# Tile 0's norm ahead of tile 1's sums, B and C from ScalarE's queue, and new prices for the planner

## The chip, the cores and the metric

The kernel runs on one core of a Trainium2 chip. The metric is the device time of one execution in microseconds (us), the median of several runs; lower is better.

## The reference

Three stages follow each other, for 4 sequences of 768 positions, in fp32:

```
# 1. scan attention, 8 heads, head size 32, state 16
la = log(clip(a)); cum = cumsum(la)             # per chunk of 32 positions
M = (C @ B.T) * exp(cum_i - cum_j) * causal
y = M @ x + (C @ state) * exp(cum)
state = exp(sum la) * state + (B * decay).T @ x
# 2. gated FFN on y (model size 256, inner size 1536)
xn = y / sqrt(mean(y*y) + 1e-6) * rms_g
z = (silu(xn @ w_gate) * (xn @ w_val)) @ w_out
# 3. channel mix on z (inner size 1024)
xk, xr = mixes of z with z one position earlier, by mu_k and mu_r
out = sigmoid(xr @ w_r) * (relu(xk @ w_k)**2 @ w_v)
```

The kernel uses chunks of 128 positions instead of 32, which gives the same sums. The weights are 64-bit floats in DRAM.

## The kernel before

**Tiles.** The 768 positions are six tiles of 128; a tile holds that stretch of all 4 sequences, so 512 columns. For each tile t the kernel runs `ffn1(t)`, the gated FFN in 12 units of 128 inner columns, and `ffn2(t - 1)`, the channel mix in 8 units; between their units it places the attention of tile t+1. Each unit of `ffn1` makes `g` and `v` (six matmuls each: weights and activations are split into a high and a low fp32r part, and `mm3` at L671 to L673 multiplies three of the four pairs), then Silu on ScalarE (`tabled`), the product `hf` on VectorE (L702), its high part by a cast on ScalarE (L137) and its low part by a subtraction on VectorE (L140). Two units later `contract` multiplies it with `w_out`. Tile 0's attention and norm have no FFN to stand beside, so they come first.

**Tile 0.** `load_a4` and `logs_e` fetch and clip `a` and take its logarithm; `sums_e(c)` on VectorE makes running sums and the small factors that `spread_e` multiplies on TensorE into a matrix of log decays (`Eb`), to which a matmul with `eye` adds the causal mask; `exp_e` takes its exponential on ScalarE (tile `E`). This is done for tiles 0 and 1 (c = 0, 1), four sequences each, two halves per sequence. `scores` multiplies C and B (L456, fp32), `masked` multiplies scores and decays (L492), `y_mm` makes y and the new state, `y_out` copies y to SBUF, `rms_sq` and `rms_mm` square it and sum over the features, `rms_a`, `rms_rest`, `rms_b` compute 1/rms on tiny tiles (Ln, Exp, Square on ScalarE, three small operations on VectorE), a matmul spreads it (L647), and `xn_f` and `xn_split` make the FFN's input `xn` and its two parts. The norm is done in two halves of 256 columns (`cols`), by `norm0`.

**Weights.** Each of 27 jobs is a block of 64-bit floats (512 KB); two jobs share a staging tile `wst` of two buffers. `convert` turns a pair into fp32r parts by bit operations: a clamp on VectorE (`move`, L260), two activations on ScalarE (`magnitude`, L265 and L267), a shift-and-or on VectorE (`merge`, L271), and per job a cast on ScalarE (L280) and a subtraction on VectorE (L281). Jobs 3q, 3q+1 and 3q+2 are w_gate, w_val and w_out for units 2q and 2q+1. `first` and `second` are jobs 0 to 3; after them `need(NEED[t][u])` places a pair before unit u of tile t as soon as that due time exceeds the number done.

**Activation tables.** Ln and Exp share one table of ScalarE, Silu and Sigmoid each have one; a switch is an instruction of its own (L124). `tabled` inserts it and chains every table function and every switch to the one before it in the program's order.

**Order.** The order on each engine is not the program's. `Order` takes all instructions, their dependencies and a price for each (`price`), and runs a list scheduler: whenever an engine is free, it takes the ready instruction that stands earliest in the program, if its buffers are free. `SIGNAL`, `LANDING` and `RATE` are its delays between engines, after a DMA, and its DMA rate in bytes per ns. The order so found is written into the program by `arrange`; on the chip each engine then runs its list in order. So a place earlier in the program is a higher rank, and a wrong price leaves an engine waiting at the head of its list. `warm_up` writes matmuls of ones that nobody reads; as they are always ready, they fill TensorE's waits.

The changed stretch of the program, before:

```
for b in range(NB): exps(0, b)
scores(0, 0); scores(0, 1)
sums_e(1)
for b in range(NB): ...       # masked, y_mm, y_out, sums of squares, state
exps(1, 0); exps(1, 1)
for s in cols: norm0(s)
for step in first: step()
exps(1, 2); exps(1, 3)
warm_up(WARM[1], pacc, "acc")
for step in second: step()
```

Of the kernel before, what the change touches and what calls it, by code (L numbers as in the profile page):

```python
# [16 lines left out]
P = 128  # L17
# [18 lines left out]
NEED = ((6, 6, 6, 10, 10, 12, 12, 14, 16, 16, 18, 18, 18),  # L36
# [7 lines left out]
WARM = (16, 24)  # L44
# [32 lines left out]
def tile_kernel(ctx: ExitStack, tc, a_c, x_t, B_t, B_s, C_s, B_p, C_p, C_h, kc,  # L77
                w_gate, w_val, w_out, w_k, w_v, w_r, out):
    nc = tc.nc
    slots, chains, groups = {}, [], []  # L80
# [38 lines left out]
    tab = [None, None]  # L119

    def tabled(out, in_, func, **kw):
        want, ins = TABLES.get(func, tab[1]), []
        if tab[1] != want:
            ins.append(lambda: nc.scalar.preload_act_table_set(want))  # L124
        ins.append(lambda: nc.scalar.activation(out=out, in_=in_, func=func, **kw))  # L125
        for make in ins:
            if tab[0] is None:
                tab[0] = make()
            else:
                nxt = make()  # L130
                chains.append((tab[0].ins.name, nxt.ins.name))
                tab[0] = nxt
        tab[1] = want

    def split(x, src, he, le):
        if he is act_e:
            nc.scalar.copy(x[:, 0, :], src)  # L137
        else:
            nc.vector.tensor_copy(x[:, 0, :], src)
        last[0] = le.tensor_tensor(out=x[:, 1, :], in0=src, in1=f32(x[:, 0, :]), op=ALU.subtract).ins  # L140

    last = [None]
# [198 lines left out]
    def sums_e(c):  # L341
        ln, w = a4[:, c], t2("hv", F32R)
# [16 lines left out]
    def spread_e(c, b):  # L359
        for half in range(2):  # L360
            ps = A[c]["Eb", b, half] = pmm.tile([P, T], F32, tag="mm", name="Eb")
# [39 lines left out]
    def load_b0():  # L401
        r = pair("xn", "Br", F32).rearrange("p a b -> p (a b)").rearrange("p (b k i) -> p b k i", b=NB, k=2)
        nc.sync.dma_start(out=r[:64], in_=B_p[0].rearrange("r b (k i) -> r b k i", k=2))
# [3 lines left out]
    def load_c0(b):  # L407
        r = A[0]["Cr", b] = rp.tile([P, 4, P], F32, tag="Cr" if b < 2 else "Br", bufs=2, name="Cr")
        nc.sync.dma_start(out=r[:64], in_=C_p[0, b].rearrange("r (k i) -> r k i", k=4))
# [173 lines left out]
    def rms_sq(c, s, he, le):  # L583
        d = A[c]
        if c <= 1:
            q = t2("sq").rearrange("p (a i) -> p a i", a=2)[:, :, :s.stop - s.start]
# [63 lines left out]
    def xn_f(c, half, s):  # L650
        d = A[c]
        f = d["xnf", half, s.start] = t2("xnf")[:, s]
# [152 lines left out]
    nc.sync.dma_start(out=k_sb, in_=kc)  # L805
    load_a4(1)
    warm_up(WARM[0], patt, "at")
    load_c0(0)
    load_b0()
    load_x(0, 1)  # L810
    load_c0(1)
    load_x(0, 0)
    load_c0(2)
    load_c0(3)
    for _ in range(2):
        w_load()
    first, second = steps(), steps()
    for c in range(2):
        logs_e(c)
# [8 lines left out]
    sums_e(0)  # L828
# [4 lines left out]

    for b in range(NB):
        exps(0, b)
    scores(0, 0)
    scores(0, 1)
    sums_e(1)
    for b in range(NB):
# [5 lines left out]
        if b % 2:  # L845
            rms_sq(0, cols[b // 2], act_e, vec_e)
            rms_mm(0, cols[b // 2])
# [403 lines left out]
```

## Time and profile before

| | |
|---|---|
| median of 3 runs | 533.36 us (530.85 to 533.69) |
| profiled execution | 529.57 us, of it span 527.8 us |
| TensorE (PE) busy | 518.5 us, 98% |
| VectorE (DVE) busy | 381.7 us, 72% |
| ScalarE (ACT) busy | 311.1 us, 59% |
| bytes moved by DMA | 42.34 MB |

Busy time of matmuls is that of pipelined records with modelled ends, so 98% does not mean that TensorE is at its peak: a 512-column matmul has a record of 0.39 us, while the next one starts 0.23 us later. L137 is line 137 of the kernel. "Idle before" in a row is the time the engine stood before it, and after the arrow what ended that.

### The profile page before, as it was taken

What the parts mean: (1) busy time and instruction counts of PE and PEld (TensorE: products, weight loads), DVE (VectorE), ACT (ScalarE), POOL (GpSimd) and SP (SyncE); (2) the same over time, 40 slices, a digit from 0 to 9 for tenths busy, and PEclk for the clock granted to TensorE, in tenths of its full rate; (3) what the DMA queues carried; (4) which work ended last, traced back from release to release, by engine and by line L of the source; (5) the groups of instructions that cost most, each with busy time, mean ns of one, the idle gap of its engine ahead of it and who ended that gap; (6) DMA issues with size and microseconds to landing.
All of it is one profiled execution on the core that took longest, in us unless ns stands there. A gap on an engine that the chain in (4) does not pass through costs nothing.

```text
span 527.8 us, 7526 instructions
## 1 busy us (share of the span) xinstructions
PE 518.5 (98%) x2872; PEld 417.9 (79%) x2872; DVE 381.7 (72%) x628; ACT 311.1 (59%) x507; POOL 13.1 (2%) x28
## 2 busy tenths in 40 slices
PE   9999999999999999999999999999999999999997
PEld 5677777788887888888888887888888888888885
DVE  7789978997969585779995687986445863335772
ACT  3698758667548954356764355874437663245552
POOL 4000000000010000001000001000000000000000
PEclk9999989999999999999999999999999999999999
DMA  7845574444151011324011324011000010000001
GB/s 214 255 147 187 195 245 160 135 145 131 55 186 39 22 51 52 108 76 154 20 45 52 105 73 145 2 40 41 0 1 1 0 40 2 0 1 0 24 18 40
DMA packets 21923, 42.34 MB, mean 80 GB/s; under 512 B 2096, under 2 KB 5168, under 8 KB 21888
## 3 DMA queue, kind: packets, MB, share of 16 engines
q1 hardware_dynamic: 19584, 33.48, 19.4%
q10 hardware_dynamic: 2304, 8.39, 4.9%
q8 instruction: 22, 0.36, 0.3%
q14 instruction: 13, 0.11, 0.1%
HBM read 38.52 MB, written 3.34 MB: 79 GB/s over the span
## 4 chain that ended last, share of the span: by engine, by line
PE 84%; DMA 5%; ACT 3%; DVE 3%; SPq 1%; issue 1%; POOL 0%; ACTq 0%; DVEq 0%
PE v L673 10%; PE v L672 10%; PE v L671 10%; PE g L671 6%; PE g L672 6%; PE g L673 6%; PE x L673 5%; PE x L671 5%; PE x L672 5%; PE kp L671 4%; PE kp L673 4%; PE kp L672 4%; DMA wst<-in_w_v 2%; PE y L505 2%; DVE E L423 2%; DMA E<-la_r 2%
## 5 line engine op out<-in xcount | busy, mean ns | idle before, releaser
L702 DVE TENSOR_TENSOR hf<-sl,v 128x512 f32<-128x512 f32 x72 | 49.2, 683 | 51.8 <-PE v L673 47.7
L137 ACT CAST h<-hf 128x512 fp32r<-128x512 f32 x72 | 44.5, 619 | 64.9 <-DVE hf L702 64.9
L125 ACT ACTIVATE sl<-g 128x512 f32<-128x512 f32 x72 | 42.6, 593 | 43.7 <-PE g L673 43.4
L140 DVE TENSOR_TENSOR h<-hf,h 128x512 fp32r<-128x512 f32 x72 | 49.4, 687 | 24.2 <-ACT h L137 24.1
L671 PE MATMUL g<-xn,wgh 128*128 128x512 f32 x144 | 58.4, 406 | 2.3 <-ACT xn L137 1.3
L672 PE MATMUL g<-xn,wgl 128*128 128x512 f32 x144 | 56.8, 395 | 0.0
L673 PE MATMUL x<-h,woh 128*128 128x512 f32 x144 | 55.6, 391 | 1.2 <-DVE h L140 1.2
L673 PE MATMUL g<-xn,wgh 128*128 128x512 f32 x144 | 56.6, 393 | 0.0
L671 PE MATMUL x<-h,woh 128*128 128x512 f32 x144 | 56.3, 391 | 0.0
L671 PE MATMUL v<-xn,wvh 128*128 128x512 f32 x144 | 56.2, 391 | 0.0
L672 PE MATMUL x<-h,wol 128*128 128x512 f32 x144 | 56.2, 390 | 0.0
L673 PE MATMUL v<-xn,wvh 128*128 128x512 f32 x144 | 56.2, 390 | 0.0
L672 PE MATMUL v<-xn,wvl 128*128 128x512 f32 x144 | 56.2, 390 | 0.0
L140 DVE TENSOR_TENSOR h<-k,h 128x512 fp32r<-128x512 f32 x48 | 32.8, 686 | 11.3 <-ACT h L137 10.8
L775 DVE TENSOR_TENSOR k<-rl 128x512 f32<-128x512 f32 x40 | 29.8, 750 | 14.7 <-ACT rl L771 14.5
L137 ACT CAST h<-k 128x512 fp32r<-128x512 f32 x48 | 29.8, 620 | 15.7 <-DVE k L775 15.5
L673 PE MATMUL v<-h,wvvh 128*128 128x512 f32 x96 | 37.6, 391 | 0.4 <-DVE h L140 0.4
L423 DVE TENSOR_TENSOR_SCAN E<-E,cmask 128x1024 f32<-128x1024 f32 x16 | 36.6, 2285 | 1.8 <-DMA E<-la_r 1.6
L671 PE MATMUL kp<-xm,wkh 128*128 128x512 f32 x96 | 37.7, 393 | 0.0
L673 PE MATMUL kp<-xm,wkh 128*128 128x512 f32 x96 | 37.4, 390 | 0.0
L672 PE MATMUL kp<-xm,wkl 128*128 128x512 f32 x96 | 37.4, 389 | 0.0
L672 PE MATMUL v<-h,wvvl 128*128 128x512 f32 x96 | 37.4, 389 | 0.0
(148 smaller groups left out, 1015.7 us busy)
## 6 DMA issues: line engine op xcount, KB each, us to landing
E<-la_r ACTq DMA_DIRECT2D x16, 512.0 KB
x<-in_x_t SPq DMA_DIRECT2D x6, 512.0 KB
wst<-in_w_gate SPq DMA_DIRECT2D x6, 512.0 KB
wst<-in_w_val SPq DMA_DIRECT2D x6, 512.0 KB
wst<-in_w_out SPq DMA_DIRECT2D x6, 512.0 KB
Br<-in_B_s SPq DMA_DIRECT2D x12, 256.0 KB
Cr<-in_C_s SPq DMA_DIRECT2D x12, 256.0 KB
out<-r SPq DMA_DIRECT2D x12, 256.0 KB
```

Source lines behind the costliest of these rows:

```text
L125: ins.append(lambda: nc.scalar.activation(out=out, in_=in_, func=func, **kw))
L137: nc.scalar.copy(x[:, 0, :], src)
L140: last[0] = le.tensor_tensor(out=x[:, 1, :], in0=src, in1=f32(x[:, 0, :]), op=ALU.subtract).ins
L423: nc.vector.tensor_tensor_scan(out=e, data0=e, data1=cmask, initial=0.0, op0=ALU.mult, op1=ALU.max)
L505: nc.tensor.matmul(y[half][32 * j:32 * j + 32, at[half]:at[half] + P], x[:, b, h * D:(h + 1) * D], m[:, h, :], start=start and at[half] == ...
L671: nc.tensor.matmul(ps, w[0][:, k, ws], x[:, 0, :], start=first, stop=False)
L672: nc.tensor.matmul(ps, w[1][:, k, ws], x[:, 0, :], start=False, stop=False)
L673: nc.tensor.matmul(ps, w[0][:, k, ws], x[:, 1, :], start=False, stop=last)
L702: nc.vector.tensor_mul(hf, sl, v)
L775: nc.vector.tensor_mul(k2, rl, rl)
```

## The change

The program around tile 0 gets another order; the planner gets other prices; some tiles other buffers. `tabled` chains a table function to its table's load only, and a load to all users of the table before it. `gates` makes every VectorE and ScalarE instruction that stands behind the early load of Silu's table wait for the last two operations of tile 0's xn.

```diff
...
-NEED = ((6, 6, 6, 10, 10, 12, 12, 14, 16, 16, 18, 18, 18),
+NEED = ((4, 4, 6, 8, 10, 12, 12, 14, 16, 16, 18, 18, 18),
         (99, 99, 99, 99, 99, 99, 99, 99, 99, 99, 99, 99, 99))
...
 MEANS = (7, 10)
-WARM = (16, 24)
+WARM = (16, 12)
...
-    tab = [None, None]
+    tab = [None, None, []]
+
+    def table(func):
+        want = TABLES.get(func, tab[1])
+        if tab[1] != want:
+            load = nc.scalar.preload_act_table_set(want).ins.name
+            chains.extend((one, load) for one in tab[2])
+            if tab[0] and not tab[2]:
+                chains.append((tab[0], load))
+            tab[:] = load, want, []
     def tabled(out, in_, func, **kw):
-        want, ins = TABLES.get(func, tab[1]), []
-        if tab[1] != want:
-            ins.append(lambda: nc.scalar.preload_act_table_set(want))
-        ins.append(lambda: nc.scalar.activation(out=out, in_=in_, func=func, **kw))
-        for make in ins:
-            if tab[0] is None:
-                tab[0] = make()
-            else:
-                nxt = make()
-                chains.append((tab[0].ins.name, nxt.ins.name))
-                tab[0] = nxt
-        tab[1] = want
+        table(func)
+        one = nc.scalar.activation(out=out, in_=in_, func=func, **kw).ins.name
+        if tab[0]:
+            chains.append((tab[0], one))
+        tab[2].append(one)
...
         if he is act_e:
-            nc.scalar.copy(x[:, 0, :], src)
+            last[1] = nc.scalar.copy(x[:, 0, :], src).ins
         else:
-            nc.vector.tensor_copy(x[:, 0, :], src)
+            last[1] = nc.vector.tensor_copy(x[:, 0, :], src).ins
         last[0] = le.tensor_tensor(out=x[:, 1, :], in0=src, in1=f32(x[:, 0, :]), op=ALU.subtract).ins
-    last = [None]
+    last = [None, None]
...
     def sums_e(c):
-        ln, w = a4[:, c], t2("hv", F32R)
+        ln = a4[:, c]
+        w = rp.tile([P, T], F32R, tag="rs", bufs=1, name="hv") if c else t2("hv", F32R)
         hi, v = w[:, :P], w[:, P:2 * P]
...
         for half in range(2):
-            ps = A[c]["Eb", b, half] = pmm.tile([P, T], F32, tag="mm", name="Eb")
+            pool, tag = (pacc, "acc") if c else (pmm, "mm")
+            ps = A[c]["Eb", b, half] = pool.tile([P, T], F32, tag=tag, name="Eb")
             nc.tensor.matmul(ps, eye, before.unsqueeze(1).broadcast_to([P, 4, P]), start=True, stop=False)
...
-    def load_b0():
+    def load_b0(q):
         r = pair("xn", "Br", F32).rearrange("p a b -> p (a b)").rearrange("p (b k i) -> p b k i", b=NB, k=2)
-        nc.sync.dma_start(out=r[:64], in_=B_p[0].rearrange("r b (k i) -> r b k i", k=2))
+        q.dma_start(out=r[:64], in_=B_p[0].rearrange("r b (k i) -> r b k i", k=2))
         for b in range(NB):
...
-    def load_c0(b):
+    def load_c0(b, q=nc.sync):
         r = A[0]["Cr", b] = rp.tile([P, 4, P], F32, tag="Cr" if b < 2 else "Br", bufs=2, name="Cr")
-        nc.sync.dma_start(out=r[:64], in_=C_p[0, b].rearrange("r (k i) -> r k i", k=4))
+        q.dma_start(out=r[:64], in_=C_p[0, b].rearrange("r (k i) -> r k i", k=4))
...
         if c <= 1:
-            q = t2("sq").rearrange("p (a i) -> p a i", a=2)[:, :, :s.stop - s.start]
+            q = rp.tile([P, T], F32, tag="Ch", bufs=1, name="sq") if s.start else t2("sq")
+            q = q.rearrange("p (a i) -> p a i", a=2)[:, :, :s.stop - s.start]
         else:
...
     nc.sync.dma_start(out=k_sb, in_=kc)
+    warm_up(WARM[0], patt, "at")
+    load_c0(0, nc.scalar)
+    load_b0(nc.scalar)
+    load_c0(1, nc.scalar)
+    w_load()
+    load_x(0, 1)
+    load_c0(2)
+    load_x(0, 0)
+    load_c0(3)
     load_a4(1)
-    warm_up(WARM[0], patt, "at")
-    load_c0(0)
-    load_b0()
-    load_x(0, 1)
-    load_c0(1)
-    load_x(0, 0)
-    load_c0(2)
-    load_c0(3)
-    for _ in range(2):
-        w_load()
+    w_load()
     first, second = steps(), steps()
-    for c in range(2):
-        logs_e(c)
+    logs_e(0)
+
     def norm0(s):
...
-    sums_e(0)
     def exps(c, b):
...
+    sums_e(0)
+    scores(0, 0)
+    scores(0, 1)
     for b in range(NB):
         exps(0, b)
-    scores(0, 0)
-    scores(0, 1)
-    sums_e(1)
     for b in range(NB):
...
             rms_mm(0, cols[b // 2])
+            norm0(cols[b // 2])
         st_up(0, b)
-    exps(1, 0)
-    exps(1, 1)
-    for s in cols:
-        norm0(s)
+    edge = [i.name for i in last]
+    logs_e(1)
+    sums_e(1)
     for step in first:
         step()
-    exps(1, 2)
-    exps(1, 3)
-    warm_up(WARM[1], pacc, "acc")
+    for b in range(NB):
+        exps(1, b)
+    table(AF.Silu)
+    here = list(nc.cur_bb.bb.instructions)[-1].name
+    gates.extend((x, here) for x in edge)
+    warm_up(WARM[1], patt, "at")
     for step in second:
...
 class Order:
-    SIGNAL, LANDING, RATE = 90.0, 1900.0, 270.0
-
-    def __init__(self, instructions, slots, chains, groups):
+    SIGNAL, LANDING, RATE = 34.0, 2100.0, 300.0
+
+    def __init__(self, instructions, slots, chains, groups, gates):
         self.slots, self.ins = slots, []
...
             self.before[b].add(a)
+        for a, b in ((where[a], where[b]) for a, b in gates):
+            for k in range(b + 1, n):
+                if self.eng[k] == self.eng[a]:
+                    self.before[k].add(a)
         self.tiles, self.touch = [[] for _ in range(n)], {}
...
         if kind == "InstDMACopy":
-            return (380.0 if e == SP_ else 100.0), 0.0, False
+            return (600.0 if e == SP_ else 100.0), 0.0, False
         if e == PE_:
...
             if x.dtype == F32:
-                part = 0.3 if aps[0].ap[0][1] <= 32 else 0.55 if x.ap[0][1] <= 64 else 1.0
-                return 20 + 1.7 * n * part, 200.0, False
-            return (228.5 if n >= T else max(n / 2.4 + 15, 45.0)), 180.0, False
+                rows, k = aps[0].ap[0][1], x.ap[0][1]
+                if k == P:
+                    return (15 + 0.32 * n if rows <= 32 else max(220.0, 20 + 1.7 * n)), 170.0, False
+                return 20 + 0.95 * n, 170.0, False
+            return (228.0 if n >= T else max(n / 2.4 + 13, 45.0)), 165.0, False
+        inputs = [a for a in i.ins if hasattr(a, "bass_ap")]
+        each = sum(columns(a) == 1 for a in inputs) if n > 1 else 0
         if e == ACT_:
-            return (1280.0, 0.0, False) if kind == "InstLoadActFuncSet" else ((60 + 0.94 * n if n > P else 250.0), 100.0, False)
+            if kind == "InstLoadActFuncSet":
+                return 1285.0, 0.0, False
+            return max((0.97 * n if kind == "InstActivation" else 32 + 0.965 * n) + 95 * each, 115.0), 98.0, False
         two = kind == "InstTensorTensor" or getattr(i, "is_scalar_tensor_tensor", False)
         if e == POOL_:
-            return (100 + 2.3 * n, 50.0, True) if kind == "InstTensorTensor" else (100 + 0.5 * n, 50.0, False)
+            return (150 + 2.5 * n, 60.0, True) if kind == "InstTensorTensor" else (80 + 0.95 * n, 60.0, False)
         if kind == "InstMemset":
             return 60.0, 30.0, False
-        psum = any(self.slots.get(a.bass_ap.tensor.name, ("",))[0] == "PSUM" for a in i.ins if hasattr(a, "bass_ap"))
+        psum = any(self.slots.get(a.bass_ap.tensor.name, ("",))[0] == "PSUM" for a in inputs)
         if getattr(i, "is_tensor_tensor_scan", False):
-            return 20 + 2.22 * n, 70.0, True
-        return 75 + (1.03 if two or psum else 0.52) * n, 75.0, not psum
+            return 48 + 2.1 * n, 82.0, True
+        return 73 + (1.035 if two or psum else 0.52) * n + 58 * each, 82.0, not psum
...
                 serial += 1
-                heapq.heappush(events, (t + self.cost[k][1] + self.SIGNAL, serial, k, [j for j in after[k] if eng[j] != e]))
+                heapq.heappush(events, (t + self.cost[k][1] + self.SIGNAL, serial, k,
+                                        [j for j in after[k] if eng[j] != e or e != PE_]))
                 for j in after[k]:
-                    if eng[j] == e:
+                    if eng[j] == e == PE_:
                         release(j)
...
```

## Rows read from the trace of the kernel before

**Rows 1.** The page's first part: busy us, share of span, instructions.

```profile
PE 518.5 (98%) x2872; PEld 417.9 (79%) x2872; DVE 381.7 (72%) x628; ACT 311.1 (59%) x507; POOL 13.1 (2%) x28
```

**Rows 2.** Stretches: length, busy us (count) by engine, granted clock, DMA share, GB/s.

```profile
0.00:5.00 5.00, 3.95 (x9) 3.14 (x10) 2.14 (x8) 1.69 (x3) 4.13 (x14) 1.00 0.29 67
5.00:10.00 5.00, 5.00 (x22) 2.84 (x20) 4.82 (x14) 0.84 (x3) 0.25 (x3) 1.00 0.98 290
10.00:15.00 5.00, 5.00 (x29) 2.47 (x30) 3.29 (x7) 3.61 (x7) 2.24 (x4) 1.00 1.00 357
39.40:64.00 24.60, 24.59 (x107) 18.14 (x108) 23.23 (x37) 19.76 (x28) 0.00 (x0) 1.00 0.62 205
72.00:74.00 2.00, 1.39 (x10) 1.08 (x9) 1.19 (x4) 1.97 (x5) 0.00 (x0) 0.90 0.88 246
74.00:77.50 3.50, 3.50 (x10) 2.84 (x11) 3.50 (x5) 1.40 (x4) 0.00 (x0) 0.57 0.96 360
```

**Rows 3.** Timeline of TensorE: start, us, line, operation, idle before.

```profile
1.05 5.92 PE L802 MATMUL warm<-ones 128*128 128x512 f32 x16 [1.05 <-DVE carry L862]
7.78 1.13 PE L456 MATMUL sc<-Cr,Br 32*128 32x256 f32 x6
14.42 0.43 PE L505 MATMUL y<-M,x 128*32 128x128 f32 x8
31.75 0.39 PE L671 MATMUL g<-xn,wgh 128*128 128x512 f32 x1
40.91 0.39 PE L671 MATMUL v<-xn,wvh 128*128 128x512 f32 x1
72.92 1.26 PE L612 MATMUL ss<-ones,sq 128*128 128x1 f32 x8 [0.61 <-ACT sq L589]
101.22 0.50 PE L671 MATMUL g<-xn,wgh 128*128 128x512 f32 x1 [1.32 <-ACT xn L137]
162.16 0.72 PE L673 MATMUL x<-h,woh 128*128 128x512 f32 x2 [1.18 <-DVE h L140]
```

**Rows 4.** Timeline of ScalarE, the same columns.

```profile
9.37 1.09 ACT L125 ACTIVATE E<-Eb 128x512 f32<-128x512 f32 x2 [4.16 <-PE Eb L363]
16.44 0.37 ACT L524 COPY yT<-y 128x256 f32<-128x256 f32 x1 [2.32 <-PE y L511]
18.59 0.63 ACT L589 ACTIVATE sq<-yT 128x512 f32<-128x512 f32 x1
25.14 0.26 ACT L125 ACTIVATE tiny<-ss,k_sb 128x2 f32<-128x2 f32 x1
28.68 1.58 ACT L137 CAST xn<-xnf 128x256 fp32r<-128x256 f32 x4 [0.18 <-DVE xnf L653]
30.16 1.08 ACT L125 ACTIVATE E<-Eb 128x512 f32<-128x512 f32 x2
32.16 2.22 ACT L267 ACTIVATE wst<-wst 128x1024 int32<-128x1024 uint32 x2
36.44 1.28 ACT L124 ACT_TABLE_LOAD   x1
37.73 0.62 ACT L280 CAST wvh<-wt 128x512 fp32r<-128x512 f32 x1
38.77 1.08 ACT L125 ACTIVATE sl<-g 128x512 f32<-128x512 f32 x2
69.74 0.34 ACTq L324 DMA_DIRECT2D E<-la_r  x1
```

**Rows 5.** Timeline of SP's queue, one issue.

```profile
3.99 0.58 SPq L320 DMA_DIRECT2D x<-in_x_t  x1
```

**Rows 6.** Timeline of VectorE.

```profile
3.04 0.91 DVE L183 TENSOR_SCALAR a<-a 128x128 f32<-128x128 f32 x1 [2.03 <-DMA a<-in_a_c]
7.76 0.42 DVE L344 TENSOR_TENSOR_SCAN a<-ones,a 128x128 f32<-128x128 f32 x1
11.19 1.28 DVE L492 TENSOR_TENSOR M<-sc,E 128x512 f32<-128x512 f32 x2
```

More of the change, by code (lines that the diff above doesn't have):

```diff
@@ L79, in tile_kernel @@
     nc = tc.nc
-    slots, chains, groups = {}, [], []
+    slots, chains, groups, gates = {}, [], [], []
     class Pool:
@@ L651, in xn_f @@
         d = A[c]
-        f = d["xnf", half, s.start] = t2("xnf")[:, s]
+        if s.start == 0:
+            d["xnf", half] = t2("xnf")
+        f = d["xnf", half, s.start] = d["xnf", half][:, s]
         nc.vector.scalar_tensor_tensor(out=f, in0=columns_of(c, s)[:, half], scalar=g_v[:, half:half + 1],
@@ L988, in tile_kernel @@
     ffn2(NC - 1, lambda *_: None)
-    arrange(tc, list(nc.cur_bb.bb.instructions), slots, chains, groups)
+    arrange(tc, list(nc.cur_bb.bb.instructions), slots, chains, groups, gates)
 ENGINES = (mybir.EngineType.PE, mybir.EngineType.DVE, mybir.EngineType.Activation, mybir.EngineType.Pool,
@@ L1200, in run, with arrange @@
         return t, order
-def arrange(tc, instructions, slots, chains, groups):
-    o = Order(instructions, slots, chains, groups)
+def arrange(tc, instructions, slots, chains, groups, gates):
+    o = Order(instructions, slots, chains, groups, gates)
     _, order = o.run()
```

## The prediction

> **What bounds the kernel now.** I read the page first: TensorE is busy 98% of the span [rows 1]. That is an average over stages with different limits, so next came the stretches [rows 2], and there the first 101 us stand apart. In all but two of these rows the clock is at its upper level, 2.4 GHz (1.00), and TensorE's records are dense, but until 31.75 us no FFN matmul runs: what fills TensorE is attention work for tile 0 and warm-up matmuls that nobody reads. The first FFN matmul starts at 31.75, and unit 2's second half, the first that needs weights of job 4, at 40.91 [rows 3]. Then I followed ScalarE through that time [rows 4]. Tile 0's exponentials start at 9.37; its norm (the `tiny` rows) waits until 25.14 behind tile 1's first exponentials; tile 1's last ones run at 30.16; three conversions' halves follow, then the switch to Silu's table at 36.44, a weight cast at 37.73, and the first Silu at 38.77. From about 25 us to there ScalarE hardly stops, so its queue sets when unit 2 can start, and TensorE's early units 0 and 1 only wait for it. Behind it VectorE is busy 23.23 of 24.60 us from 39.4 to 64 [rows 2]: little room there for work pushed later. Past 101 us TensorE is the limit; I found single stops before 101.22 (1.32 us) and 162.16 (1.18 us) [rows 3]. So only the first 101 us, with some 8 to 10 us of slack, can change much.
>
> **The change part by part.** The sum is against the profiled execution, 529.57 us (span 527.8 and 1.8 around it); the median of the three timed runs, 533.36, lies 3.8 above it. I carry the difference over to the median.
>
> *Loads.* B and C of tile 0 (C0, B0, C1: 512 KB) move from SP's queue to ScalarE's, and go out at once; SP sends two 512 KB weight blocks ahead of x. An issue on SP at the start took 0.58 us [rows 5], one on ScalarE's queue later 0.34 [rows 4]: three cost ScalarE 1.0 to 1.7 us ahead of its table load of 1.28, which then ends by 0.73+1.7+1.28 = 3.7. The first Ln waits for a clip on VectorE that began at 3.04 and took 0.91 [rows 6], so it starts at 3.95 at the earliest: the issues are hidden, and without that cover cost at most 1.7. x lands later: 67 GB/s over the first 5 us are 335 KB, then it ran at 290 GB/s, later 357 [rows 2]; 2.18 MB stand up to the end of x where 1.07 MB did, which makes 10.2 to 11.4 us instead of 7.5. The first matmul that reads x ran at 14.42 [rows 3] and in the new order may want it at about 12, so: nothing, at most 0.5 us. B's early landing is worth nothing by itself, since the 16 warm-up matmuls hold TensorE until 6.8 [rows 3].
> The DMA engines' share was 0.98 to 1.00 from 5 to 15 us [rows 2], on one queue. The Trainium skill, "DMA: Bandwidth & Descriptors", section "Issuing engines are not separate DMA queues", says that a second issuing engine only saves issue time because all queues share the 16 engines; the full share agrees, and it speaks against this part of the change: by it, and by the rows alike, the loads' term is zero.
>
> *Scores ahead of the exponentials, tile 1's sums behind.* Two blocks of scores at about 1.06 us each (six of their eight records took 1.13 with the pipeline's tail [rows 3]) now run right after the warm-up: 6.8+2.1, plus four fills of 0.23, gives 9.9, and the first exponential starts at 10.3, not 9.37. That is 0.9 lost. VectorE's second round of sums, from 7.76, ended only where the first masking product starts, at 11.19 [rows 6]; they go behind, so the first product follows its exponential at about 10.9. Masking itself thus hardly starts earlier, but its four pairs need not wait for scores again.
>
> *Norm first, then the table, then the rest.* No instruction vanishes; ScalarE's order does. I add up what ScalarE must do from tile 0's first exponential to the cast of job 4's weights, by [rows 4]: 16 exponentials at 0.54 (8.6), 4 copies of y at 0.37, 2 squares at 0.63, 6 small norm steps at 0.26, the xn casts 1.58, 6 conversion halves at 1.11 (6.7), 5 weight casts at 0.62 (3.1), the table 1.28: 25.6. About 17 of these are single records that overlap their neighbour by some 0.09 (two exponentials take 1.08, one 0.60): 24.1. Before, that list ran from 9.37 to 38.35, 29.0 us, so 4.9 us were idle. Now the Silus of units 0 and 1 (1.08) and their two casts (1.1) come ahead of job 4, because the due times move jobs 4 and 5 from unit 0 to unit 2: 24.1+2.2 = 26.3. From 10.3 that gives 36.6 plus idle time, and the subtraction on VectorE 0.7: unit 2's second half at 37.3 plus idle, against 40.91. With no idle time 3.6 are gained; with 4.9 again, 1.3 are lost. I take 0.9 idle, nearer the lower end, since the table-function chain that forced the old order is gone (Ln and Exp wait now only for their table load) and tile 1's exponentials and conversions can fill the norm's gaps: **-2.7**. The FFN itself may start at about 25 instead of 31.75, which by itself is worth nothing: units 0 and 1 then wait for Silu.
>
> *Gates.* VectorE's and ScalarE's work listed after the early table load now waits for tile 0's last xn. Behind it stand the state products, tile 1's decay clip, scan and product, some 3.5 us that VectorE did at 17 to 26. They fall into the stretch where VectorE had 1.4 us free in 24.6 [rows 2]. Much of it is due only with tile 1's y around 68; I price it at nothing, up to 3.5 (the rival below).
>
> *Prices.* The planner's order changes everywhere. Visible targets: the half-speed stretch 74 to 77.5, clock 0.57, costs 3.5x0.43 = 1.5, with 0.2 more in 72 to 74 [rows 2], and the wait of 0.61 before the sums of squares at 72.92 [rows 3] in front of it: 2.3 together. ScalarE had put a conversion half ahead of the copy and square these sums need. Truer prices may take that away or make another such place, 0 to -2.3, or +2.3 in the worst case: **-1.5**. Of the two later stops (2.5), which hang on a 2.3 us scan and a late load, I count **-0.7** (0 to -2.5). The smaller second warm-up (12 for 24) takes nothing from the path; its matmuls only filled waits. The tiles that get other buffers remove waits I see none of: nothing either way.
>
> Sum: -2.7-1.5-0.7 = **-4.9**: 524.7 for a profiled execution like this one, **528.5** against the median.
>
> **The rivals.**
> *A larger gain.* ScalarE without idle time (-3.6), the 72 to 77.5 place gone whole (-2.3) and both later stops gone (-2.5): -8.4, 525.0. For it: nothing but order stands in the way, and nothing past 162 us can add. Against: VectorE would have to run nearly solid from 11 to 90 us.
> *Given back in VectorE.* The 3.5 us behind the gate come due in the saturated stretch and push hf, h and weight subtractions in full: -4.9+3.5 = -1.4, 532.0, no change. For it: 94% busy at 39 to 64. Against: what the gate holds back is mostly due only with tile 1's y, and ScalarE, not VectorE, ended the waits before 40 us.
> *Slower: job 4 too late.* The conversion of jobs 4 and 5, demoted to unit 2, starts only after unit 1's h. If ScalarE idles 4.9 as before, the first Silu comes at 10.3+26.3-2.8-2.2+4.9 = 36.5, h of unit 1 is cast at about 39.5, and then 1.11+1.11+1.22+0.62+0.69 = 4.8 follow in line: second half of unit 2 at 44.4, +3.5. TensorE has then stood for most of 30 to 44 us with two units done, its clock falls, and a stretch like 74 to 77.5 costs 1.5. With -2.2 of the other terms: +2.8, 536.2. It decides if that matmul starts past about 42. For it: the due time was 6 and is 4. Against: staging is free early and the planner fills idle slots with any conversion that is ready.
> The clock fell here after a stretch of small matmuls and a wait under 1 us [rows 2, 3]. The Trainium skill, "TensorE: Matmul & The Clock Gate", section "What's actually happening", calls the low level the default that activity releases; the trace bears that out at 74 us, where by the rule alone a longer wait as in this rival would make a fall likelier.
>
> **How the numbers follow.** Forecast 0.50 (its own range 525.8 to 530.7), larger gain 0.14, given back 0.21, slower 0.15. Half a percent is 2.7 us, about what a measurement of this kernel can tell from no change. Faster 0.50+0.14 = 0.64, same 0.21, slower 0.15. The range takes the unknowns in: down past the larger gain's 525.0 by the timed runs' own spread (2.8) and some, 521.5, since new prices touch every stage, and up to the slower case, 536.5.
>
> **What would show it.** Right: the `tiny` rows on ScalarE before tile 1's exponentials and before 21 us; first FFN matmul at 24 to 27; the Silu table load before the second conversion and ending by 33; unit 2's second half at 37 to 39; no clock of 0.57 in the 65 to 75 us region; tile 1's first FFN matmul at 95 to 98 instead of 101.22. Wrong: a first Silu past 36, a new half-speed stretch before 45 us, VectorE at 95% with TensorE waiting for h between 38 and 62, or stops past 101 us that sum to more than before.

## The result and the profile after

The changed kernel takes 525.86 us, median of four runs (524.75 to 526.59), against 532.49 (530.85 to 533.69, four runs) for the kernel before: ratio 0.9876, 95% interval [0.9839, 0.9912], 6.6 us or 1.2% faster. The kernel before scatters more than the changed one: in three later comparisons its medians were 528.26, 530.23 and 529.68, and the changed kernel, run again beside the second of them, took 524.87, ratio 0.9905 [0.9882, 0.9928]. So the gain is 1.0 to 1.2%, 5 to 7 us. The two profiled executions, 526.23 and 529.57, lie 3.3 apart (spans 524.1 and 527.8); the accounts below are between these two.

The total came out about as forecast (528.5). The way there did not: the FFN started later, not earlier, and the gain came behind it. The page's first and second part after (busy us and share by engine; granted clock in 40 slices, in tenths), which answer to [rows 1]:

```profile
PE 516.0 (98%) x2860; PEld 416.8 (80%) x2860; DVE 379.0 (72%) x628; ACT 307.1 (59%) x507; POOL 11.5 (2%) x28
...
PEclk9889999999999999999999999999999999999999
```

TensorE's busy share is the same 98%. The second and third slice of the clock hold what is new. Stretches of the changed kernel, with the columns of [rows 2]:

```profile
22.80:29.60 6.80, 6.48 (x20) 4.41 (x20) 3.82 (x10) 3.48 (x10) 0.00 (x0) 0.50 0.55 207
...
39.40:64.00 24.60, 24.60 (x113) 18.67 (x111) 24.35 (x41) 19.30 (x29) 0.00 (x0) 1.00 0.79 259
...
74.00:77.50 3.50, 3.50 (x19) 2.44 (x19) 3.05 (x5) 3.17 (x4) 0.00 (x0) 1.00 0.90 317
```

From 22.8 to 29.6 us TensorE ran at its lower level, 1.2 GHz (0.50), where the kernel before ran at 2.4 GHz; at 74 to 77.5 the old half-speed stretch is gone. From 39.4 to 64 VectorE is now busy 24.35 of 24.60 us, and TensorE does not wait at all. TensorE's timeline (start, us, line, operation, idle before), the answers to [rows 3]:

```profile
21.90 0.83 PE L617 MATMUL ss<-ones,sq 128*128 128x1 f32 x6 [1.37 <-ACT sq L594]
...
29.05 0.89 PE L652 MATMUL ss<-tiny 128*128 128x128 f32 x4
...
33.18 0.39 PE L678 MATMUL g<-xn,wgh 128*128 128x512 f32 x1
...
38.75 1.13 PE L460 MATMUL sc<-Cr,Br 32*128 32x256 f32 x6
...
40.86 0.73 PE L678 MATMUL x<-h,woh 128*128 128x512 f32 x2
...
43.03 0.39 PE L678 MATMUL v<-xn,wvh 128*128 128x512 f32 x1
...
98.08 0.50 PE L678 MATMUL g<-xn,wgh 128*128 128x512 f32 x1 [0.37 <-ACT xn L139]
...
158.26 0.73 PE L680 MATMUL x<-h,woh 128*128 128x512 f32 x2 [0.46 <-DVE h L142]
```

The first FFN matmul is at 33.18 (before 31.75, +1.4), the first that needs job 4 at 43.03 (before 40.91, +2.1), tile 1's first at 98.08 (before 101.22, -3.1). So 4.6 us are won between the two. Most of it is lost time that is gone: a stop of 0.96, one of 0.61, 1.7 in the half-speed stretch, and the stop before tile 1's first matmul fell from 1.32 to 0.37. The first of these stood, in the kernel before, here:

```profile
39.41 0.50 PE L671 MATMUL g<-xn,wgh 128*128 128x512 f32 x1 [0.96 <-ACT sl L125]
```

A further 0.7 goes at the next one, 1.18 to 0.46. Together -3.9, where the spans differ by 3.7. In the changed kernel's second run that last stop was 1.14, so its 0.7 belongs to one execution.

Why the start is late stands in the waits. ScalarE after, which answers to [rows 4], and VectorE after:

```profile
9.91 4.03 ACT L132 ACTIVATE E<-Eb 128x512 f32<-128x512 f32 x8 [5.15 <-PE Eb L367]
...
20.02 0.26 ACT L132 ACTIVATE tiny<-ss,k_sb 128x2 f32<-128x2 f32 x1 [1.21 <-PE ss L617]
...
20.51 0.21 ACT L132 ACTIVATE tiny<-tiny 128x2 f32<-128x2 f32 x1
20.62 0.61 ACT L282 CAST wgh<-wt 128x512 fp32r<-128x512 f32 x1
21.12 0.20 ACT L132 ACTIVATE tiny<-tiny 128x2 f32<-128x2 f32 x1
21.23 0.62 ACT L594 ACTIVATE sq<-yT 128x512 f32<-128x512 f32 x1
...
33.65 1.28 ACT L124 ACT_TABLE_LOAD   x1
...
35.98 0.58 ACT L132 ACTIVATE sl<-g 128x512 f32<-128x512 f32 x1
```

```profile
6.17 0.35 DVE L349 SCALAR_TENSOR_TENSOR hv<-hv,k_sb,a 128x128 fp32r<-128x128 f32 x1 [0.70 <-DMA k_sb<-in_kc]
...
21.36 0.16 DVE L643 SCALAR_TENSOR_TENSOR tiny<-tiny 128x2 f32<-128x2 f32 x1
21.44 0.68 DVE L352 TENSOR_TENSOR wvvh<-hv,k_sb 128x512 fp32r<-128x512 f32 x1
22.04 0.15 DVE L644 SCALAR_TENSOR_TENSOR tiny<-tiny 128x2 f32<-128x2 f32 x1
...
26.94 0.16 DVE L644 SCALAR_TENSOR_TENSOR tiny<-tiny 128x2 f32<-128x2 f32 x1
29.98 0.87 DVE L660 SCALAR_TENSOR_TENSOR xnf<-yT,k_sb,ss 128x256 f32<-128x256 f32 x2 [2.87 <-PE ss L652]
```

The norm did come forward: its first `tiny` step is at 20.02, not 25.14. But between its small steps (0.15 to 0.26 us each) stands work of lower rank: a weight cast of 0.61 on ScalarE at 20.62, tile 1's factor products of 0.68 on VectorE at 21.44. The second half's squares are held behind the cast until 21.23, TensorE waits 1.37 us for them, and the clock falls at 22.8. At half speed TensorE's work for the norm and for tile 1's decays takes about twice as long (a pair of `Eb` matmuls 0.88 us, at full speed 0.46); VectorE has the second half's 1/rms at 27.10, but the matmul that spreads it stands behind others in TensorE's list and starts at 29.05.

### The profile page after: what moved, and what is told of

Same layout as the page of the kernel before. It is cut to its first block, busy times and chain, and to the rows that moved or that the text cites. A ratio compares the mean times of both kernels' runs of the same rounds, so it can differ in the third digit from the quotient of the medians.

```text
span 524.1 us, 7504 instructions
## 1 busy us (share of the span) xinstructions
PE 516.0 (98%) x2860; PEld 416.8 (80%) x2860; DVE 379.0 (72%) x628; ACT 307.1 (59%) x507; POOL 11.5 (2%) x28
## 4 chain that ended last, share of the span: by engine, by line
PE 94%; DVE 3%; DMA 1%; ACT 1%; issue 0%; ACTq 0%; DVEq 0%
PE v L680 10%; PE v L678 10%; PE v L679 10%; PE g L678 7%; PE g L679 6%; PE g L680 6%; PE x L680 6%; PE x L678 6%; PE x L679 6%; PE kp L678 4%; PE kp L680 4%; PE kp L679 4%; PE y L509 2%; PE sc L460 2%; PE warm L809 2%; DMA E<-la_r 1%
## 5 line engine op out<-in xcount | busy, mean ns | idle before, releaser
L680 PE MATMUL v<-h,wvvh 128*128 128x512 f32 x96 | 37.5, 390 | 0.8 <-DVE h L142 0.8
L778 ACT ACTIVATE rl<-kp 128x512 f32<-128x512 f32 x48 | 28.6, 595 | 15.3 <-PE kp L680 14.8
L678 PE MATMUL v<-h,wvvh 128*128 128x512 f32 x96 | 37.4, 389 | 0.0
```

The source lines that it names most:

```text
L678: nc.tensor.matmul(ps, w[0][:, k, ws], x[:, 0, :], start=first, stop=False)
L680: nc.tensor.matmul(ps, w[0][:, k, ws], x[:, 1, :], start=False, stop=last)
L778: nc.scalar.activation(out=rl, in_=kp, func=AF.Relu)
```

## The experiments

Each kernel ran beside the kernel before on the same chip. "The new program" is the change without its class `Order`; "old prices" are that class's numbers and delays as they were before, the gates kept. The expectations use letters for theories, each stated there: P is about the new prices, C about TensorE's clock at the start, R about the planner's release of work on the same engine; O, N and T are rivals. The kernel before has another median in each comparison, so a difference between two kernels that did not run side by side is given by the medians and by the ratios. All in one table (times of TensorE's first FFN matmul, unit 2's second half, tile 1's first FFN matmul, the largest stop between 145 and 165 us, from the profiled execution; - is none over 0.3 us):

```
kernel                       median  ratio [95%]              FFN    v2     tile 1  stop  span
before                       532.49                           31.75  40.91  101.22  1.18  527.8
after                        525.86  0.9876 [0.9839, 0.9912]  33.18  43.03   98.08  0.46  524.1
after again                  524.87  0.9905 [0.9882, 0.9928]  32.58  42.41   97.48  1.14  523.0
new prices alone             530.82  1.0028 [0.9998, 1.0059]  33.74  41.53   96.80  4.12  530.0
new program, old prices      520.24  0.9822 [0.9788, 0.9855]  27.88  40.59   93.32  0.97  519.5
 the same again              520.97  0.9843 [0.9812, 0.9875]  28.29  41.00   93.70  0.39  519.2
after, B and C on SP         525.88  0.9934 [0.9904, 0.9964]  32.58  42.69   98.31   -    523.0
after + eight fills          524.06  0.9895 [0.9864, 0.9926]  31.66  41.91   96.86   -    522.7
after, old release           522.97  0.9853 [0.9818, 0.9888]  31.07  42.51   96.37   -    522.0
old prices, new release      525.53  0.9917 [0.9887, 0.9946]  31.87  41.73   97.02  1.60  523.2
old prices, norm late        523.47  0.9871 [0.9843, 0.9899]  29.24  38.75   95.73   -    519.8
after, old release + fills   529.27  1.0004 [0.9979, 1.0030]  30.40  41.42   96.25  2.56  523.6
old prices, old due times    532.56  1.0058 [1.0037, 1.0079]  28.57  38.82   96.88  5.56  528.3
old prices, no gates         522.65  0.9870 [0.9841, 0.9900]  28.70  40.10   94.28  0.82  520.5
```

**New prices alone.** The kernel before with the new class `Order`, nothing else.

```diff
-    SIGNAL, LANDING, RATE = 90.0, 1900.0, 270.0
+    SIGNAL, LANDING, RATE = 34.0, 2100.0, 300.0
...
+ every line of the change in class Order, with an empty list of gates
```

> The kernel before, with only the planner's class from the kernel after (new prices, delays and the release of dependents on the same engine); program, loads, due times and table chain are the old ones. Theory P (the gain comes from truer prices, which take the stops at 38 us, 72 us with the half-speed stretch behind it, and 99.6 us out of tile 0's FFN): the first FFN matmul stays near 31.75 us, the way from it to tile 1's first FFN matmul falls from 69.5 us to about 65, and the median falls by 4 to 6 us against before. Rival O (the stops went because the new program order shifts what meets what): within 1.5 us of before, a clock of about 0.6 still somewhere between 60 and 80 us.

Measured 530.82 (528.88 to 532.18): no gain. The stops at 39, 73 and 101 us and the half-speed stretch at 74 are gone in its trace too, 6.4 us less between first FFN matmul and tile 1's. The start is 2.0 later, and a new stop of 4.12 us comes at 161.69. Its chain of waits there (start, us, what):

```profile
148.39 9.74 DMA Ch<-in_C_h
...
158.16 0.69 DVE Ch L418
158.85 0.33 DVE E L423
...
160.97 0.68 DVE h L140
...
161.69 1.22 PE x L673 x2
```

VectorE's list has a product for tile 2's attention (`Ch`) and a long running sum (`E`) ahead of the subtraction that makes `h`; the load of `Ch` took 9.74 us, and the FFN waits behind it. In this stop the clock falls too, to 0.50 from 160.43 to 167.26; 5.6 us of that lie behind the stop and cost half as much, 2.8 us. So -6.4 meets +2.0 at the start, +2.9 at the stop (4.12 for 1.18), +2.8 by the clock and +0.4 in a later stop: +1.7, where the spans differ by 2.2. P's first part came true, the way from the first FFN matmul to tile 1's is 63.1 us; its gain of 4 to 6 us did not come. Rival O had the time right, but its sign, a low clock between 60 and 80 us, is missing.

**The new program under the old prices.**

```diff
-    SIGNAL, LANDING, RATE = 34.0, 2100.0, 300.0
+    SIGNAL, LANDING, RATE = 90.0, 1900.0, 270.0
...
- every other price and the release of the change
+ those of the kernel before
```

> The kernel after, with the planner's old prices, delays and same-engine release; program order, loads, due times, gates and table chain are the new ones. Theory P: 4 us or more slower than after (530 to 533), with one or more stops of over 0.8 us between 35 and 100 us. Rival O: within 1.5 us of after (524.5 to 527.5).

Measured 520.24 (519.83 to 521.31), and 520.97 (520.02 to 521.88) when run again: the fastest kernel of this study, 3.9 to 5.6 us below the change itself by the medians, 0.3 to 0.8% by the ratios. Neither P (530 to 533) nor O (524.5 to 527.5) named so short a time. The FFN starts at 27.88, 5.3 earlier than after, and the spans differ by 4.6: the start is the whole difference. Its ScalarE, its VectorE and its TensorE:

```profile
19.37 0.26 ACT L132 ACTIVATE tiny<-ss,k_sb 128x2 f32<-128x2 f32 x1 [0.88 <-PE ss L617]
19.66 0.44 ACT L132 ACTIVATE tiny<-tiny 128x2 f32<-128x2 f32 x2
```

```profile
20.27 0.15 DVE L643 SCALAR_TENSOR_TENSOR tiny<-tiny 128x2 f32<-128x2 f32 x1
20.46 0.16 DVE L644 SCALAR_TENSOR_TENSOR tiny<-tiny 128x2 f32<-128x2 f32 x1
...
25.55 0.87 DVE L660 SCALAR_TENSOR_TENSOR xnf<-yT,k_sb,ss 128x256 f32<-128x256 f32 x2
```

```profile
27.88 0.39 PE L678 MATMUL g<-xn,wgh 128*128 128x512 f32 x1
...
40.59 0.50 PE L678 MATMUL v<-xn,wvh 128*128 128x512 f32 x1
...
93.32 0.50 PE L678 MATMUL g<-xn,wgh 128*128 128x512 f32 x1
```

Here the small steps follow each other: the two on ScalarE in one go at 19.66, the last two on VectorE at 20.27 and 20.46 where the changed kernel has them at 21.36 and 22.04. The clock stays at 1.00. And the first matmul of job 4 hardly moved against the kernel before, 40.59 for 40.91, while the time fell by 8.

**B and C back on SP's queue.**

```diff
-    load_c0(0, nc.scalar); load_b0(nc.scalar); load_c0(1, nc.scalar)
+    load_c0(0); load_b0(nc.sync); load_c0(1)
```

> The kernel after, with B and C of tile 0 issued on SP's queue in the same places of the program. Theory (the loads' term is zero, since the scores hold TensorE anyway): within 1 us of after; the small constants land earlier, so VectorE's wait of 0.70 us for k_sb at 6.17 goes, and the first exponential still starts at 9.5 to 10.5 us. Rival (the early B and C are what lets the scores run at 7.3 us): the scores start after 8 us, the exponentials after 11, and the time is 1 to 3 us longer.

Measured 525.88 against 525.86 and, in the second run of the change, 524.87. By the ratios (0.9934 against 0.9876 and 0.9905) it is 0.3 to 0.6% slower, and the intervals overlap: nothing clear of noise, but not shown to be zero. Of the theory's signs, the wait for `k_sb` is gone; but the scores start at 8.67 instead of 7.32 and the exponentials at 11.13 instead of 9.91, as the rival said. The Trainium skill, "DMA: Bandwidth & Descriptors", section "Issuing engines are not separate DMA queues", says that loads run on the same 16 DMA engines whichever engine starts them, and that a second issuing engine only saves issue time; this run agrees, since what ScalarE's queue gained is that the three issues began 1.36 us earlier (0.74 for 2.10). A half-speed stretch, of 3.4 us, and the late start stay.

**Eight fills for TensorE's wait.** The matmuls of ones that nobody reads, placed behind tile 0's attention.

```diff
     edge = [i.name for i in last]
+    warm_up(8, pacc, "acc")
```

> The kernel after, with 8 more matmuls of ones, ranked behind tile 0's norm and ahead of tile 1's sums, in a PSUM buffer of the pool acc. Theory C (the first FFN matmul came at 33.18 instead of the forecast 24 to 27 in part because the clock fell to half from 22.8 to 29.6 us after TensorE's wait of 1.76 us at 20.1): the fill runs in that wait, the clock stays at its upper level, the first FFN matmul comes at 30 to 31.5 us and the time falls by 1 to 3 us against after. Rival (the clock was a symptom; VectorE's and ScalarE's lists set the start): the first FFN matmul stays within 0.7 us of 33.18, time within 0.7 us of after, whatever the clock does.

Measured 524.06 (523.06 to 524.74). The clock stays at 1.00, and the first FFN matmul comes at 31.66, 1.5 earlier than in the profiled execution of the change and 0.9 earlier than in that of its second run; the span is 1.4 and 0.3 shorter. So the half clock cost some 1 to 1.5 us of the 5.3 by which the start is later than under the old prices. In the total that is not clear of noise (ratio 0.9895 against 0.9876 and 0.9905). The rest is not the clock: the squares were even later, at 21.95.

**The change once more.** The changed kernel as it is, beside the three runs that follow.

> The kernel after once more, unchanged, beside the runs below. Every theory: 524.5 to 527; first FFN matmul at 32 to 34 us.

It took 524.87, with the half-speed stretch at 21.5 to 28.3.

**The old release in the changed kernel.** The changed planner makes work on the same engine wait for its operand's delay, as other engines do; the old one let it start at once.

```diff
-    [j for j in after[k] if eng[j] != e or e != PE_]))
+    [j for j in after[k] if eng[j] != e]))
...
-    if eng[j] == e == PE_:
+    if eng[j] == e:
```

> The kernel after, with all its prices and delays, but in the planner's run an instruction's followers on the same engine are free at once again, as before. Theory R (it is this delay of 0.13 us behind each step that makes the planner put a cast of 0.5 us or a conversion between the three small steps of a norm, so the norm's second half comes some 3 us later): the small steps stand back to back again, the first FFN matmul comes at 27 to 29.5 us, and the time is 519 to 522. Rival N (the prices of single operations order the start): the first FFN matmul stays past 31 us and the time within 1.5 us of after's 525.9.

Measured 522.97 against 524.87 beside it: 1.9 of the 3.9 to 5.6 us, and the FFN starts at 31.07, not in the 27 to 29.5 that R asked for. The small steps do stand together again (two on ScalarE in one go at 20.48, two on VectorE at 21.03 and 21.22), but the clock falls here too, to 0.50 from 23.14 to 26.56, after a wait of 0.52 us at 21.44. R holds in part.

**The new release under the old prices.** The same lines the other way round.

```diff
-    [j for j in after[k] if eng[j] != e]))
+    [j for j in after[k] if eng[j] != e or e != PE_]))
...
-    if eng[j] == e:
+    if eng[j] == e == PE_:
```

> The kernel of run e2 (after's program with the old prices and delays), with only the same-engine delay of the new planner. Theory R: first FFN matmul past 30.5 us, 523.5 to 526.5. Rival N: within 1.5 us of e2's 520.2, first FFN matmul before 29.5 us.

Measured 525.53 (524.27 to 527.24), ratio 0.9917 where the same kernel with the old release has 0.9822 and 0.9843: these lines alone cost 4.6 to 5.3 us by the medians, 3.9 to 5 by the ratios, as R asked. Its ScalarE, VectorE, TensorE and one stretch:

```profile
19.77 0.21 ACT L132 ACTIVATE tiny<-tiny 128x2 f32<-128x2 f32 x1
19.91 0.63 ACT L594 ACTIVATE sq<-yT 128x512 f32<-128x512 f32 x1
20.45 0.19 ACT L132 ACTIVATE tiny<-tiny 128x2 f32<-128x2 f32 x1
```

```profile
20.95 0.69 DVE L352 TENSOR_TENSOR wvvh<-hv,k_sb 128x512 fp32r<-128x512 f32 x1
21.55 0.15 DVE L643 SCALAR_TENSOR_TENSOR tiny<-tiny 128x2 f32<-128x2 f32 x1
...
21.95 0.15 DVE L644 SCALAR_TENSOR_TENSOR tiny<-tiny 128x2 f32<-128x2 f32 x1
```

```profile
20.59 1.34 PE L617 MATMUL ss<-ones,sq 128*128 128x1 f32 x8 [0.62 <-ACT sq L594]
...
31.87 0.39 PE L678 MATMUL g<-xn,wgh 128*128 128x512 f32 x1
```

```profile
21.20:28.00 6.80, 6.64 (x22) 4.78 (x23) 5.22 (x15) 4.47 (x11) 0.00 (x0) 0.50 0.70 249
```

The two steps that ran in one go are apart, with the squares between them; VectorE's come at 21.55 and 21.95, behind 0.69 us of tile 1's products. TensorE waits 0.62 us for the squares, and from 21.2 to 28.0 its clock is at 0.50. In the planner the new release puts a delay between two dependent steps of one engine, `SIGNAL` and a part of the price: 0.12 to 0.13 us in the changed kernel (34 ns and 82 to 98), 0.17 to 0.19 in this one with the old prices (90 ns and 75 to 100). A list scheduler that takes whatever is ready fills it with 0.6 us of something else.

**The norm ranked late, under the old prices.**

```diff
-            norm0(cols[b // 2])
         st_up(0, b)
-    edge = [i.name for i in last]
     logs_e(1); sums_e(1)
+    exps(1, 0); exps(1, 1)
+    for s in cols: norm0(s)
+    edge = [i.name for i in last]
     for step in first: step()
-    for b in range(NB): exps(1, b)
+    exps(1, 2); exps(1, 3)
```

> The kernel of run e2 with tile 0's norm ranked behind tile 1's sums and its first four exponentials, as before; loads, table chain, gates, buffers and due times as in e2. Theory (the norm's rank is what brings the FFN forward): the first FFN matmul at 30 to 32.5 us and 3 to 4 us slower than e2, 523 to 525. Rival (the loosened table chain, the sums' place and the gates do it, the rank of the norm little): within 1 us of e2.

Measured 523.47 (521.74 to 524.25), ratio 0.9871, 0.3 to 0.5% above the norm in front; the intervals overlap. The FFN starts only 1.4 later, below what was expected; unit 2's second half is even earlier, 38.75. So the norm's rank is worth perhaps 1.5 to 2.5 us here. But the edit hardly moves the norm: its first `tiny` step runs at 19.81 here and at 19.79 in the second run of the kernel with the norm in front, where the kernel before has it at 25.14 and the new prices alone at 26.91. What frees it must be another part of the new program; the loosened chain of table functions is the likely one, since the old chain put tile 1's exponentials ahead of the norm's Ln. No run takes that chain back by itself, so this is not shown.

**The control, and both repairs of the start together.** First the new program with the old prices again:

> The kernel of run e2 (after's program with the old prices, delays and release) unchanged, beside the three below. Every theory: 519.5 to 522, first FFN matmul before 29.5 us.

It stands in the table. Then the changed kernel with the old release and the eight fills:

> Run e5 (new prices, old same-engine release) with the 8 filling matmuls of run e4. Theory R+C (release and clock explain the start together): the clock stays up, the first FFN matmul comes at 28.5 to 30 us, 1 to 2 us before e5's 31.07, and the time is 520 to 522. Rival (the prices of single operations still cost something at the start): first FFN matmul past 30.5 us although the clock stays up.

Measured 529.27 (525.37 to 531.88), although the FFN starts at 30.40, earlier than in either repair alone, and the clock stays at 1.00. The profiled execution took 525.37 and has a stop of 2.56 at 156.72, again behind the load of `Ch`. The other eleven executions have no trace, but their mean granted clock is on record: 0.990 to 0.997, where the profiled one has 1.000. So each of them ran for some time at the lower level; where, and whether this stop brings it, is not shown. The repairs of the start thus don't add up to the kernel with the old prices, and why stays open.

**The old due times, under the old prices.**

```diff
-NEED = ((4, 4, 6, 8, 10, 12, 12, 14, 16, 16, 18, 18, 18),
+NEED = ((6, 6, 6, 10, 10, 12, 12, 14, 16, 16, 18, 18, 18),
```

> Run e2 with the old due times, so jobs 4 and 5 are ranked before unit 0 again. The forecast's step (the second half of unit 2, which needs job 4, sets how far the FFN gets): it comes at 37 to 39 us instead of 40.59 and the time falls by 1.5 to 2.5 us. Rival T (TensorE fills the wait for job 4 with scores and contractions, so only its lost time counts): it comes earlier, and the time stays within 1 us of c2.

Measured 532.56 (530.47 to 534.14), 11.6 above the control, with the FFN's start unmoved (28.57 and 28.29) and unit 2's second half 2.2 earlier, at 38.82. The forecast's step asked for a gain of 1.5 to 2.5 us, rival T for the control's time within 1 us; neither came. Tile 1's first FFN matmul is 3.2 later than in the control: the time goes in stops of 0.86 at 36.61 and 1.60 at 48.87, and above all at 159.89. Chain of waits and stretch of this kernel there:

```profile
147.02 10.85 DMA Ch<-in_C_h
...
157.89 0.03 DVE Ch L422
...
158.50 0.69 DVE hf L709
...
159.22 0.63 ACT h L139
...
159.89 0.79 PE x L678
```

```profile
159.60:163.00 3.40, 3.11 (x7) 2.48 (x8) 3.40 (x4) 2.39 (x5) 0.00 (x0) 0.50 0.02 6
```

`hf` stands behind the `Ch` product on VectorE, and the load of `Ch` took 10.85 us. TensorE stood 5.56 us, and its clock fell for 3.4 more. The same rows of the kernel with the new due times, in its first and in its second run:

```profile
142.52 7.18 DMA Ch<-in_C_h
```

```profile
143.50 7.34 DMA E<-la_r
```

In the first the load took 7.18 and the stop was 0.97; in the second another load ended the wait, and the stop was 0.39. Which part of the 11.6 belongs to the due times as such, and which to the accident of what the list holds at 147 us, stays open.

**No gates, under the old prices.**

```diff
-    gates.extend((x, here) for x in edge)
+    gates.extend((x, here) for x in edge[:0])
```

> Run e2 without the gates, so work listed behind the table load may run before tile 0's last xn. Forecast's pricing (nothing): within 1 us of c2. Rival (the gates keep conversions of over 1 us out of the norm's way): the first FFN matmul 1 us or more later than c2's, and 1 to 3 us slower.

Measured 522.65 (521.03 to 523.03) against 520.97 (520.02 to 521.88): the gates are worth some 1.7 us, though the two ratios' intervals overlap. The FFN starts at 28.70, only 0.4 later than in the control, where the rival asked for 1 or more: how the gates help is not shown.

## Why the prediction was right in its total and wrong in its steps

**The total.** -4.9 was forecast against the median, -5 to -7 was measured. As shares of the profiled pair: +1.4 at the start, -4.6 from there to tile 1, -0.7 behind it. The start was to give -2.7 and the rest -2.2; that the total fitted is luck, since a start that lost and stops that gave more than twice what was forecast made up for each other.

**"Norm first, then the table, then the rest" (-2.7): the step that failed.** It had two errors. The first: "From 10.3 that gives 36.6 plus idle time" adds ScalarE's work as if its order were free. ScalarE's idle time between the first exponential (9.91) and the cast of job 4's weights (40.55) was taken as 0.9 us; in the trace it is 6.5, more than the 5.1 that the same count gives before, and under the old prices it is still 4.8. The new order holds the squares and the small steps apart by one cast and VectorE's products, and TensorE's wait for them brings the half clock; unit 2's second half came at 43.03, not 37.3 to 38.2. The half clock was one of the signs named as proof against the forecast, and it came. The second error matters more: "which by itself is worth nothing" of an earlier FFN, and with it the choice of unit 2's second half as what sets the end. Under the old prices the FFN started 3.9 earlier than before, job 4's first matmul 0.3 earlier, and the span fell by 8.3. With the old due times job 4 came 2.2 earlier than in the control, tile 1's first FFN matmul 3.2 later, and the span grew by 9.1. TensorE fills the wait for job 4 with scores of tile 1 and `w_out` matmuls of tile 0 that must be done anyway (38.75 and 40.86 above); what counts is the time in which it does nothing of use: its start, its stops and its half clock. The traces bear this out: from the first FFN matmul to tile 1's, without TensorE's idle time and half of the time at half speed, it is 63.1 to 65.4 us in all fourteen, and 423.9 to 425.4 us behind that. The work is nearly the same everywhere; the lost time is what differs.

**"Prices" (-1.5 and -0.7).** The place at 72 to 77.5 did go, whole (-2.3), the later stops by 1.7 (by 1.0 in the second run), and one at 39.41 of 0.96 that the forecast had not listed. But the credit is not the prices': the same stops are gone under the old prices, and with the prices alone other losses take all of it back. It seems that they hung on one particular list, and each of these two other lists loses them. Beside the new program the prices cost 3.9 to 5.6 us by the medians; the release is the part shown to do it by itself, and about 3 us of start remain with the old release (31.07 against 27.88). Up to 1.7 of them can be that run's 3.4 us at half speed; the rest lies in price numbers that were not taken apart.

**The signs.** Of those named, one came true, that the clock of 0.57 at 65 to 75 us is gone, and tile 1's first FFN matmul came close (98.08 and 97.48 in the two runs, where 95 to 98 was named). The `tiny` rows came by half: the first half's begin at 20.02, but the second half's run from 23.86 to 26.43, among tile 1's exponentials. The first FFN matmul (33.18 for 24 to 27), Silu's table (loaded by 34.93, not 33) and unit 2's second half did not, and the first Silu at 35.98 stands just at its limit of 36. Good signs from 65 us on beside bad ones in the first 45 say by themselves that the gain did not come from the start.

**"Loads" (0).** Not refuted: 525.88 against 525.86 and 524.87, up to 0.6% by the ratios. Its parts were off: an issue on ScalarE's queue took 0.59 to 0.62 us at the start, not 0.34, VectorE waited 0.70 for `k_sb`, and the early landing, called worth nothing by itself, let the scores start 1.35 earlier. The first exponential came at 9.91, not 10.3.

**"Gates" (0, at most +3.5).** Worth some -1.7 under the old prices. VectorE became as full as feared, 24.35 of 24.60, and TensorE waited for nothing in that stretch: "given back in VectorE" fell.

**The smaller warm-up and the other buffers (0).** Neither was run by itself. Eight more warm-up matmuls did not put the FFN's start off (31.66), which fits that they fill waits.

**The rival "slower: job 4 too late".** Its sign came true, 43.03 is past its 42, and so did a half-speed stretch, though at 22.8 and not in its place at 30 to 44; its price did not, for the reason of the second error.

## What to carry to other kernels

When one engine is busy 98% of the time, count its own lost time (late start, stops, half clock) and not the arrival of one input that it can work around. Test a planner's truer price on the chip alone and with the program it is meant for: here more detailed numbers made a worse order, in part because a short delay between small dependent steps invites a long step in between. And a new order can lose elsewhere by accident: look for loads that start and land late, and for what stands behind their users in an engine's list.

## What the runs showed of the hardware

The clock did not go by the length of the wait alone. It fell to half after waits of 0.52 (old release, at 21.44), 0.61 [rows 2, 3], 0.62, 1.37 and 1.63 us (B and C on SP, at 22.73) around the sums of squares and other small matmuls, and in waits of 4.12 and 5.56 us among 512-column matmuls. It stayed at 1.00 through 1.47 (norm late, at 47.38), 1.60 (new release, at 157.33) and 2.56 (both repairs, at 156.72) among those, and once through 0.52 in front of sums of squares (B and C on SP again, at 72.84).

One 256 KB load (`Ch`) took 7.18, 9.74 and 10.85 us from its issue to its landing in three kernels, with 2.25 MB of other loads issued between 140 and 160 us; and one and the same program had another load land last in another execution. Kernels with a stop of over 2 us behind it scattered by 3.3 to 6.5 us (the new prices alone, the old due times, both repairs), the fastest kernel by 1.5 to 1.9. But the kernel before, with 1.18 us there in its trace, scattered by 6.3 and 6.8 us in two comparisons.

What its scatter does go with is the clock. In all 44 executions of the kernel before in the three later comparisons, those with a mean granted clock of 0.996 to 1.000 took 526.35 to 529.40 us, those with 0.993 or 0.994 took 529.68 to 531.51, and those with 0.990 took 532.70 to 533.17. So how often or how long the clock falls differs between executions of one program.
